# Moving the first loads of three phases of a training-step kernel into the last step of the phase before

## The chip, the cores and the metric

The kernel runs on one core of one Trainium2 chip. The metric is device time in microseconds (us), lower is better. Executions of one kernel spread by 10 to 20 us here (0.3 to 0.6%), so ratios come with a 95% interval and small claims rest on several executions. The engines are TensorE (PE in the profile, PEld for its weight loads), VectorE (DVE), ScalarE (ACT), GpSimd (POOL) and SyncE (SP).

## The reference, cut to what matters

The kernel computes the forward output and all gradients of one block: attention over segments with a memory carried from segment to segment, and a gated linear unit (GLU), both modulated by six vectors made from `c`.

```python
# 2048 rows of 512, 32 heads of 128, segments of 32 rows with 8 memory rows, F = 1792
for s in range(64):                                  # sequential
    h = concat([mem, xs]); q, k, v = h @ Wq, h @ Wk, h @ Wv
    o = softmax(mask(q @ k.T * scale)) @ v @ Wo
    mem = o[:8]; outs.append(o[8:])
x = x + ga * attention;  h = layernorm(x) * (1 + cb) + sb
x = x + gb * ((sigmoid(h @ w_gate) * (h @ w_up)) @ w_down)
# ... and jax.vjp of all of it for grad_out: 11 gradients
```

## The kernel before

The phases that matter here: phase 2 is the forward recurrence (64 steps), phase 3 the GLU as a pipeline of seven stages over 16 blocks of 128 rows, followed by the GLU's weight gradients (14 chunks of dW_down, then dW_gate and dW_up). Phase 4 is the backward recurrence, phase 5 the remaining weight gradients, beginning with the one of Wo. I call the handovers seam 1 (phase 2 to the GLU), seam 2 (GLU pipeline to its weight gradients) and seam 3 (phase 4 to 5).

```python
# start of the GLU (seam 1); tiles lie in memory that phase 2 has given back
nc.sync.dma_start(w_down[:], ...)                    # 1.83 MB, as w_up and w_gate
ga_bc, sb_bc, cb1_bc, gb_bc = ...                    # four broadcasts of 256 KB
...
load(0)                                              # row block 0: ten small loads on SP
nc.sync.dma_start(w_up[:], ...); nc.sync.dma_start(w_gate[:], ...)
load(1)
self.run_pipeline(NT, [s0, s1, s2, s3, s4, s5, s6], deepest_first=True)
...
# weight gradients (seam 2)
nc.sync.dma_start(dbr[:], self.DBROWS...)            # rows of d(block), 2.1 MB
for fc in range(FC):                                 # 14 chunks of 16 matmuls
    if fc % 3 == 0: hr = ...; nc.sync.dma_start(hr[...], self.HHROWS...)
    ...
# phase 5 (seam 3)
for tl in range(2):
    q = (nc.sync, nc.scalar)[tl]
    q.dma_start(rows_a[...], self.OSR...)            # 0.64 MB
    q.dma_start(dyrows[...], self.DAROWS...)         # 1 MB
    for tp_ in range(M // 2): q.dma_start(dyrows[...], DHA piece)
    q.dma_start(dyrows[last row], zrow)              # a row of zeros
```

The softmax here doesn't subtract the row's maximum and nothing guards it: scores larger than these inputs give would overflow.

## Time and profile before

| measured | before |
|---|---|
| median of 3 runs | 3368.5 us (3366.07 to 3373.47) |
| PE busy | 3056.8 us, 91% of the span |
| DVE, ACT, POOL busy | 49%, 36%, 31% |
| bytes moved by DMA | 692.22 MB, mean 205 GB/s |
| mean granted TensorE clock | 0.980 |

PE fills the kernel. The few dips lie at the seams, and the change addresses just those. The views that show it stand in the prediction. In the instruction view the bracket at the end of a line is the idle time of that engine just before the instruction, and what ended it.

### The profile page before, as it was taken

How to read it: one execution, taken by the hardware profiler on the slowest of the kernel's cores; microseconds unless marked ns; L12 is line 12 of the kernel's file. 1: busy time of each engine (PE TensorE's matmuls, PEld its weight loads, DVE VectorE, ACT ScalarE, POOL GpSimd, SP SyncE). 2: the span in 40 equal slices, each digit the busy share in tenths (PEclk: the TensorE clock that was granted, in tenths of full speed). 3: DMA queues.
4: the chain of work that ended last, by engine and by line, in shares of the span. 5: the costliest groups of instructions: out<-in, count | busy, mean ns of one | idle time of the engine just before them, and what ended most of it. 6: DMA issues, size and time to landing. Idle time of an engine off the chain costs nothing. (4 is left out here: it accounts for less than half of the span.)

```text
span 3368.5 us, 97290 instructions
## 1 busy us (share of the span) xinstructions
PE 3056.8 (91%) x39586; PEld 1793.4 (53%) x39662; DVE 1649.4 (49%) x4158; ACT 1225.1 (36%) x2842; POOL 1060.2 (31%) x2262
## 2 busy tenths in 40 slices
PE   6999999998998689978989999999999978999999
PEld 3566656565565444435555555555555543445454
DVE  5566666666665677633244455555544541322221
ACT  3454544444444333312134444444444430100111
POOL 2344433333343355530122222222222221322321
PEclk8999999999999899989999999999999998999999
DMA  8777787778777888877769999999999998777686
GB/s 281 154 168 161 165 156 163 155 158 157 155 162 154 215 204 206 197 214 248 229 178 242 240 245 236 250 244 242 246 240 244 241 235 226 236 195 210 179 225 164
DMA packets 862317, 692.22 MB, mean 205 GB/s; under 512 B 562198, under 2 KB 737574, under 8 KB 861740
## 3 DMA queue, kind: packets, MB, share of 16 engines
q1 hardware_dynamic: 768156, 503.74, 66.8%
q0 software_dynamic: 39488, 135.58, 12.0%
q10 hardware_dynamic: 54224, 46.66, 5.3%
q8 instruction: 312, 5.11, 0.6%
q14 instruction: 137, 1.12, 0.1%
HBM read 292.29 MB, written 275.02 MB: 168 GB/s over the span
## 5 line engine op out<-in xcount | busy, mean ns | idle before, releaser
L1584 PE MATMUL gps<-rows,hrows 128*128 128x512 bf16 (+2 forms) x2124 | 415.1, 355 | 1.9
L1584 PEld LDWEIGHTS <-hrows 128*128 128x128 bf16 x2160 | 211.2, 98 | 204.2
L222 PEld LDWEIGHTS <-hT 128*32 128x32 bf16 x6144 | 180.5, 98 | 174.1 <-issue 41.2
L65 POOL COPY vT<-b_colsv 128x24 bf16<-128x24 bf16 (+2 forms) x256 | 49.5, 238 | 577.6 <-DMA VT<-vT 569.1
L63 DVE CAST ot<-gps 128x512 bf16<-128x512 f32 (+3 forms) x77 | 48.9, 635 | 359.7 <-PE gps L1584 210.8
L272 DVE TENSOR_TENSOR dh_lo<-dh_ps,dh_hi 128x256 bf16<-128x256 f32 x128 | 48.3, 419 | 316.2 <-ACT dh_hi L268 316.2
L61 ACT ACTIVATE ot<-gps 128x512 bf16<-128x512 f32 (+3 forms) x77 | 42.5, 551 | 389.2 <-PE gps L1584 278.6
L737 POOL TENSOR_TENSOR Pst<-Pst,rden 120x1408 bf16<-120x1408 bf16 x64 | 162.3, 2535 | 36.3 <-POOL hT L481 20.7
L1588 POOL DMA_DIRECT2D out_dram<-ot x108 | 81.2, 752 | 290.3 <-DVE ot L63 155.2
L222 PE MATMUL pass_ps<-Wv,hT 128*32 128x512 bf16 x2048 | 127.2, 391 | 29.7 <-ACT hT L731 29.7
L1317 POOL DMA_DIRECT2D DVR<-rows_x x64 | 34.5, 540 | 371.6 <-DMA rows_x<-dVT 371.6
L222 PE MATMUL pass_ps<-WoT,dyT 128*32 128x512 bf16 x2048 | 125.1, 386 | 27.9 <-ACT dyT L1400 26.9
L61 ACT ACTIVATE dQT<-g_ps 128x512 bf16<-128x512 f32 (+1 forms) x192 | 94.0, 562 | 151.4 <-issue 146.5
L1594 PE MATMUL gps5o<-dyrows,rows 128*128 128x512 bf16 x588 | 134.5, 387 | 0.8 <-issue 0.2
L651 DVE TENSOR_TENSOR Ost<-or_ps,rden 120x512 bf16<-120x512 f32 (+1 forms) x192 | 124.3, 647 | 19.6 <-PE dc_ps L628 0.5
L1296 DVE SCALAR_TENSOR_TENSOR dS<-dp_ps,Pst_l 128x512 bf16<-128x512 f32 (+1 forms) x192 | 118.2, 643 | 24.1 <-PE dp_ps L1294 19.5
L222 PE MATMUL pass_ps<-Wk,hT 128*32 128x512 bf16 x2048 | 124.4, 383 | 0.0
L222 PE MATMUL pass_ps<-Wq,hT 128*32 128x512 bf16 x2048 | 122.4, 379 | 0.0
L211 PE MATMUL at_ps<-Wo,OT 128*32 128x512 bf16 x2048 | 122.3, 380 | 0.0
L211 PE MATMUL dh_ps<-WkT,dKT 128*32 128x512 bf16 x2048 | 122.3, 380 | 0.0
L211 PE MATMUL dh_ps<-WvT,dVT 128*32 128x512 bf16 x2048 | 122.2, 380 | 0.0
L211 PE MATMUL dh_ps<-WqT,dQT 128*32 128x512 bf16 x2048 | 121.6, 379 | 0.0
(383 smaller groups left out, 7106.9 us busy)
## 6 DMA issues: line engine op xcount, KB each, us to landing
OSR<-Ost SPq DMA_DIRECT2D x64, 352.0 KB
OT<-OT SPq DMA_DIRECT2D x64, 352.0 KB
PS<-Pst SPq DMA_DIRECT2D x64, 352.0 KB
OT_l<-OT SPq DMA_DIRECT2D x64, 352.0 KB
Pst_l<-PS SPq DMA_DIRECT2D x64, 352.0 KB
DVR<-rows_x POOLq DMA_DIRECT2D x64, 352.0 KB, 4.3
DKR<-rows_x POOLq DMA_DIRECT2D x64, 352.0 KB, 4.9
DQR<-rows_x POOLq DMA_DIRECT2D x64, 352.0 KB, 3.6
```

Of the source, the lines that this page charges most:

```text
L61: return nc.scalar.activation(out, in_, AF.Copy)
L63: return nc.vector.tensor_copy(out, in_)
L65: return nc.gpsimd.tensor_copy(out, in_)
L211: self.nc.tensor.matmul(ps[32 * j:32 * j + 32, :], lhsT=lhsT, rhs=w, start=(n < 4), stop=(n >= total - 4), tile_position=(0, 32 * j))
L222: self.nc.tensor.matmul(ps[32 * j:32 * j + 32, :], lhsT=lhs(c), rhs=rhs, start=(c == 0), stop=(c == DC - 1), tile_position=(0, 32 * j))
L272: nc.vector.tensor_tensor(lo[:], ps[:, 256 * h:256 * h + 256], parts[h][:], op=ALU.subtract)
L651: nc.vector.tensor_tensor(part3(Ost, pi)[0:120, 0:n, :], or_ps[0:120, 0:n, :], rden[:, pi * PG:pi * PG + n].unsqueeze(2).to_broadcast([120 ...
L737: nc.gpsimd.tensor_tensor(Pst[0:120, :, :], Pst[0:120, :, :], rden[:, :].unsqueeze(2).to_broadcast([120, G, 128]), op=ALU.mult)
L1296: nc.vector.scalar_tensor_tensor(out=part3(dS, pi), in0=ps[:, 0:n, :], scalar=cfg.scale, in1=part3(Pst, pi), op0=ALU.mult, op1=ALU.mult)
L1584: nc.tensor.matmul(ps[:, 0:ng * E], lhsT=hrows[:, tp_, c * 128:(c + 1) * 128], rhs=rows[:, tp_, 0:ng * E], start=(tp_ == 0), stop=(tp_ == ...
L1588: nc.gpsimd.dma_start(outw[c * 128:(c + 1) * 128, h0:h0 + 3 * (ng - 1) + 1:3, :], ot[:, 0:ng * E].rearrange("p (h e) -> p h e", e=E))
L1594: nc.tensor.matmul(ps[:], lhsT=rows[:, tp_, gg * E:(gg + 1) * E], rhs=dyrows[:, tp_, :], start=(tp_ == 0), stop=(tp_ == NTP - 1))
```

## The change

Its intent: no phase should begin with PE waiting for a first load. It lays the new phase's tiles over tiles of the old one that die early in its last step (`flat` makes such a view), and issues the loads as soon as the last reader is done. The core of the diff, cut:

```diff
# phase 2, last step: the GLU's weights over Wv and Wk
+                if s == NS - 1:                          # after the v projection
+                    nc.sync.dma_start(self.w_up, ...)
+                    self.mod_bc(None, 2, ...); self.mod_bc(None, 3, ...)
...
+                if s == NS - 1:                          # after the k projection
+                    nc.sync.dma_start(self.w_down, ...); self.mod_bc(None, 4, ...)
...
+                if s == NS - 1:                          # after q, k, v are turned
+                    self.mod_bc(None, 5, ...); nc.sync.dma_start(self.w_gate, ...)
...
+                if s == NS - 1:
+                    self.glu_first = self.glu_load(0, nc.scalar)    # row block 0 on ACT's queue
# GLU: three chunks of dW_down beside the drain of the pipeline
+            def after(it):
+                if it == NT + 1: nc.scalar.dma_start(dbr, ...)      # over w_gate and w_up
+                elif it == NT + 2: load_hr(0)
+                elif NT + 3 <= it < NT + 6: wd_chunk(it - NT - 3, ...)
# phase 4, last step: rows of phase 5 over WoT
+                if s == 0:
+                    self.p5_first()      # rows_a and the DAROWS part of dyrows, all on SP
...
             store_rows_x(0)
+            self.p5_second()             # the eight DHA pieces; zero rows stay in phase 5
```

## The prediction

> **What bounds the kernel now.** I read the page first: the busy slices show a kernel that TensorE (PE) fills, with a few dips, and each dip lies where one phase hands over to the next. The two lines that carry this are
>
> ```profile
> PE   6999999998998689978989999999999978999999
> PEclk8999999999999899989999999999999998999999
> ```
>
> A slice is 3368.5 / 40 = 84.2 us. Slice 13 (1095 to 1179 us) has PE at 6 and a lower granted clock: the handover from the forward recurrence (phase 2) to the GLU (phase 3). The handover from the GLU pipeline to its weight gradients (1477 to 1504) lies at the edge of slices 17 and 18, and that from the backward recurrence (phase 4) to the last weight gradients (phase 5) in slice 32 or 33. The change touches nothing else, so I went next to the engines' busy time in just those stretches:
>
> ```profile
> core 0: us, PE busy (x) PEld busy (x) DVE busy (x) ACT busy (x) POOL busy (x), PEclk, DMA share, GB/s
> 1109.00:1122.00 13.00, 5.41 (x52) 4.98 (x53) 3.84 (x11) 1.83 (x2) 1.64 (x3) 0.61 0.84 277
> 1122.00:1139.00 17.00, 9.11 (x128) 8.47 (x126) 11.38 (x19) 9.17 (x10) 3.63 (x5) 0.80 0.77 271
> 1170.00:1440.00 270.00, 248.12 (x1223) 116.58 (x1235) 186.01 (x314) 91.50 (x165) 153.54 (x161) 0.98 0.82 202
> 1477.00:1504.00 27.00, 8.10 (x45) 3.55 (x45) 8.65 (x16) 3.85 (x6) 6.67 (x9) 0.75 0.98 297
> 2769.00:2787.00 18.00, 0.41 (x2) 0.17 (x3) 0.80 (x5) 0.00 (x0) 0.54 (x1) 0.55 1.01 191
> 2787.00:2830.00 43.00, 37.13 (x151) 15.81 (x154) 7.21 (x15) 2.49 (x4) 6.63 (x11) 0.87 1.00 273
> ```
>
> In the steady GLU stretch (third row) PE works 248 of 270 us. In the handovers no compute engine is the bound; the DMA engines are (share 0.77 to 1.01), and PE waits for a first load. The instructions in order of time name each wait; the number in brackets is PE's idle time just before the line.
>
> ```profile
> 1117.52 5.41 PE L803 MATMUL tp<-ident,w_down 128*128 128x128 bf16 x56 [6.83 <-DMA w_down<-in_B_w_down_dram]
> 1129.38 4.19 PE L792 MATMUL tp<-ident,w_up 128*128 128x128 bf16 x48 [6.45 <-DMA w_up<-in_B_w_up_dram]
> 1139.16 0.93 PE L878 MATMUL mm<-w_gate,hdT 128*128 128x448 bf16 x4 [1.17 <-DMA hdT<-h]
> ...
> 1490.58 0.60 PE L979 MATMUL tp<-ident,da 128*128 128x128 bf16 x4 [5.29 <-DVE da L966]
> 1492.59 0.59 PE L975 MATMUL acc_ps<-pr_ga,ones 128*32 128x512 bf16 x1 [1.42 <-POOL pr_ga L969]
> 1503.99 12.34 PE L1024 MATMUL gps<-dbr,hr 128*128 128x512 bf16 x47 [10.78 <-DMA hr<-HHROWS]
> ...
> 2786.59 1.86 PE L1594 MATMUL gps5o<-dyrows,rows5a 128*128 128x512 bf16 x4 [17.60 <-DMA dyrows<-zrow]
> ```
>
> The sums: seam 1 has 6.83 + 6.45 + 1.17 = 14.5 us of waiting; seam 2 has 1.36 (before s5 of the last row block, for its transposed du) + 5.29 + 1.42 + 10.78 = 18.9; seam 3 has 17.6. Together 51.0 us, 1.5% of the time. That is the ceiling for waits alone.
>
> **What the Trainium skill says.** "TensorE: Matmul & The Clock Gate", section "What's actually happening": PE's default state is throttled, it falls back after an idle window of about 3.4 us and needs about as long of work to be released. The trace agrees: after the 17.6 us wait the granted clock is 0.55 and the first gradient matmuls run slowly. 47 recorded (48 issued) matmuls take 12.34 us after the wait at 1504, where a later run takes 4.48 us for 20, so 48 warm ones would take about 10.5. Each wait of over 4 us thus costs near 2 us more, and new waits would too. "DMA: Bandwidth & Descriptors", section "Queues, rings and completion order": each DMA engine consumes one queue's descriptors in ring order and takes turns between queues. So an early bulk load stands ahead of everything issued later on the SP queue. That agrees with w_up and w_gate: issued at 1121.9 and 1122.4, they landed at 1129.4 and 1134.2, one after the other, 3.67 MB in 12.3 us = 298 GB/s. I use that rate below. No page I found gives the wait I see on SP itself: its 9th transfer (1117.49) is issued only when the first of the eight before it (w_down) has landed, and the 10th when the second has. I take a depth of eight as this trace's behaviour.
>
> **The change, part by part.**
>
> *Seam 1.* The three GLU weights (1.83 MB each) and four 256 KB broadcasts are issued in the last step of phase 2, over Wv, Wk, Wq as soon as that step's projections have read them; row block 0 comes over the ACT queue. Removed: the waits on w_down and w_up. Not removed: the 168 transposes of the weights, which become PE's own limit. 112 of them took 1129.4 to 1138.0 = 8.6 us with both weights there; the other 56 are half, 4.3. From PE's last work of phase 2 (1110.7) this gives 1110.7 + 12.9 = 1123.6 at the earliest for the first GLU matmul, against 1139.16. A second chain is worse. The softmax transpose of the last step (Pst, issued at 1099 and landed by 1105.9) now goes into the SP queue behind the weights. From w_up's issue at about 1093: 5.5 + 1.0 + 0.9 MB (that step's own stores) at 298 GB/s = 25 us, so Pst lands near 1118 to 1121. GpSimd is held to program order there: the 2.5 us normalisation of Pst, three row stores (0.58 + 1.07), then rstd of block 0 (0.56), then VectorE's three operations to h2 (0.55 + 0.69 + 0.69), then the transposing DMA (issued at 1136.57, used at 1139.16: 2.6). Sum from 1119.5: 2.5 + 1.7 + 0.6 + 1.9 + 2.6 = 9.3, so 1129. Gain between 15.6 and 10; ten DMA issues on ScalarE (0.4 to 0.5 us each) before its last fold evictions cost up to 2. I take **10**.
>
> *Seam 2.* Three of the 14 dW_down chunks (48 matmuls) move into the drain of the pipeline, with dbr and the first hr group loaded over the dead w_gate and w_up from about 1454 on. Warm they take 10.4 us. Chunk 0 fits before s5(15), chunk 1 in the 5.3 us wait for da, chunk 2 after the last sums. Chunk 0 takes 3.5 us where only 1.4 was idle, so s5(15) and what hangs on it slip about 2 us. The next group hr(1) lies over cb1 and the a_rows ring, so it can't be issued before GpSimd's pr_ga(15) has read a_rows: 1492.5 + 2 to 3.5. It then needs the 8.1 us that hr(0) needed (1495.90 to 1503.99). So chunk 3 starts at about 1503 to 1504, where chunk 0 stands now; the three chunks' 12.2 us are gained, but the cold start (about 1.9) is paid again there. Gain **10**.
>
> *Seam 3.* rows_a and the DAROWS part of dyrows (2 x 0.64 + 2 x 1 MB) are issued at the start of step 0 over WoT, the eight DHA pieces at its end, and only two zero rows are left. Before, these stood behind the out_dram stores on SP (which wait for dh_rb at 2767) and behind each other. 3.4 MB from 2743.5 at 298 GB/s end at 2755; the DHA pieces follow by about 2765, the zero rows before 2770. PE ends phase 4 at 2769. Against me: the step's rows_x transpose now queues behind 2 MB, GpSimd's tail copies wait behind its store, and the tail's matmuls (2759.3) may slip 2 us. Start about 2771 instead of 2786.6, a gain of 15.5, plus some of the 2.2 us of cold clock (40 matmuls in 10.84 us, 8.65 warm). But 2787 to 2830 runs with DMA at share 1.00, and PE waits 4.78 us in it for a load. Only the 3.4 MB moved out (11 us), plus loads that can be issued sooner, speed that stretch. I count **14**.
>
> After each seam the kernel runs on PE as before, so the gains add: 10 + 10 + 14 = 34 us, 3368.5 - 34 = **3334 us** (0.990).
>
> **Rivals.** (a) *All waits vanish with the cold clocks*: 51 + about 6 gives 3311. For it: PE is the bound elsewhere (413 us busy of the 415 from 2945 on). Against it: the rings lie over live buffers (hr(1)), and the weight transposes are work. (b) *The moved loads only change places*: Pst and rows_x behind bulk transfers hold up GpSimd, and seams 1 and 3 gain 3 and 8. With 8 at seam 2 that is 3349. For it: DMA at 0.84 to 1.11 around all seams. Against it: rows_x and Pst feed no matmul of their own step. (c) *Overlaid views make false waits in the GLU's steady loop*, since the rings and w_down share one tensor: if loads waited for all readers of Wk, a row block (20 us) would grow by several us, and 16 of them by 50 or more: about 3385. Against it: the kernel before already fills and reads parts of tiles such as dyrows independently.
>
> **Range and chances.** Central 3334; (a) and (b) set the range, 3317 to 3353. A gain of 2% needs 67 us, more than all waits and cold clocks counted here, so faster gets 0.03; (c) or an upset instruction order gives slower 0.02; within 2% 0.95.
>
> **What would show it.** Right: waits on w_down and w_up gone and the first w_gate matmul 12 to 15 us after PE's last phase-2 work was due, or later with hdT, rstd or Pst named (the second chain); three dW_down chunks between 1477 and 1500 and a wait on hr of 4 to 7 us after them; the wait before the first gps5o under 4 us. Wrong: PE's time per GLU row block off 20 us, the stretch after gps5o's start losing what the start won, or any seam gaining under 4 us.

## More of the kernel before

The builder schedules: within one engine it may emit an instruction earlier than its place in the source where its data allow it. The recurrences are pinned to program order, the rest is not.

## The result, and the profile after

| | before | changed |
|---|---|---|
| median in the same rounds | 3370.54 us (4 runs) | 3357.61 us (3355.77 to 3365.03, 4 runs) |
| ratio | 1 | 0.9967, 95% interval 0.9947 to 0.9986 |
| profiled execution: span, clock | 3368.5, 0.980 | 3355.7, 0.983 |

A ratio here is the mean time of one kernel's fast runs over that of the other's fast runs of the same rounds, so it is not quite the ratio of the medians. The class "within 2%" was right, the number was not: 34 us were predicted, 13 came by the medians, and the time lies above the range's end of 3353.

The same two rows of the page of the changed kernel (40 slices of the span, busy tenths of PE and the granted clock in tenths):

```profile
PE   6999999999998699988989999999999988999999
PEclk8999999999999899999999999999999998999999
```

The dip at slice 17 is nearly gone (slices 16 to 19 read 9789 before and 9889 now), the one in slice 13 is still a 6, and seam 3 shows as two 8s in slices 32 and 33. So one seam of three looks mended. Busy time per stretch of the changed kernel, with stretches chosen to answer to those shown of before:

```profile
1106.00:1120.00 14.00, 0.00 (x0) 0.00 (x0) 0.43 (x1) 0.30 (x2) 0.00 (x0) 0.63 0.89 302
1120.00:1141.00 21.00, 14.37 (x179) 12.76 (x180) 15.65 (x29) 11.49 (x14) 11.29 (x12) 0.83 0.59 164
1485.00:1512.00 27.00, 18.54 (x100) 8.39 (x100) 8.90 (x17) 4.75 (x8) 8.40 (x12) 0.95 0.98 287
2752.00:2776.00 24.00, 7.67 (x106) 3.20 (x106) 1.51 (x6) 0.66 (x2) 4.27 (x9) 0.70 0.99 195
2776.00:2820.00 44.00, 39.22 (x160) 16.65 (x161) 8.41 (x20) 2.20 (x4) 5.54 (x9) 0.89 1.00 251
```

Columns: stretch, length, busy time and instructions of PE, PEld, DVE, ACT and POOL, then granted clock, DMA share, GB/s. First row: for 14 us at seam 1 the compute engines do almost nothing (PE 0, VectorE 0.43, ScalarE 0.30 us), while the DMA engines run at 302 GB/s. Third row: PE now works 18.5 of 27 us at seam 2, where before it worked 8.1. Last two rows: seam 3 still has the DMA engines at a share of 0.99 and 1.00, as before (1.01 and 1.00). PE's waits in order of time:

```profile
1120.14 0.21 PE L281 MATMUL ao_b_ft<-foldsel,ao_b_hi 128*128 128x32 bf16 x1 [14.81 <-ACT ao_b_hi L268]
...
1140.79 1.67 PE L909 MATMUL mm<-Wv,hdT 128*128 128x448 bf16 x4 [3.70 <-DMA hdT<-h]
...
1485.74 3.63 PE L1031 MATMUL mm<-Wv 128*128 128x512 bf16 x16 [0.98 <-DMA Wv<-HHROWS]
...
1512.20 5.41 PE L1031 MATMUL gps<-Wv,Wk 128*128 128x512 bf16 x16 [7.18 <-DMA Wk<-HHROWS]
...
2762.43 3.22 PE L211 MATMUL dh_tps<-WvT,dh_tail 128*32 128x512 bf16 x32 [10.60 <-POOL dh_tail L1732]
...
2776.37 11.66 PE L1673 MATMUL gps5o<-WoT 128*128 128x512 bf16 x40 [4.67 <-DMA WoT<-zrow]
...
2792.44 26.23 PE L1673 MATMUL gps5o<-WoT,rows 128*128 128x512 bf16 x113 [4.41 <-DMA rows<-OSR]
```

**Seam 1.** The waits for w_down and w_up are gone, and a new one of 14.81 us stands before phase 2's own last folding: PE waits for ScalarE. (w_gate shows as Wv, since it lies there.) Why ScalarE and GpSimd were late is in their own lines, from two views of that kernel, ScalarE's first (`db` is a product of the GLU's first blocks, `rstd` a factor of the layer norm, which `hdT` needs):

```profile
1104.76 0.41 ACTq L788 DMA_DIRECT2D Wk<-in_grad_out_dram  x1
1107.83 0.56 ACTq L319 DMA_DIRECT2D Wk<-AOA  x1
1113.45 0.28 ACTq L320 DMA_DIRECT2D Wk<-AOB  x1
1116.76 0.30 ACTq L319 DMA_DIRECT2D Wk<-AOA  x1
...
1119.70 0.66 ACT L268 ACTIVATE ao_b_hi<-ao_tps 128x256 bf16<-128x256 f32 x2 [17.48 <-DMA Wk<-AOB]
```

```profile
1126.81 2.53 POOL L760 TENSOR_TENSOR Pst<-Pst,rden 120x1408 bf16<-120x1408 bf16 x1 [21.67 <-DMA Pst<-ET]
...
1130.95 2.65 POOL L865 TENSOR_TENSOR db<-Wk,Wq 128x512 bf16<-128x512 bf16 x2
...
1134.68 0.58 POOL L878 TENSOR_TENSOR rstd<-ve,mhalf 128x1 f32<-128x1 f32 x1
```

The ten loads of row block 0 take ScalarE 0.3 to 0.6 us each to issue, but between the first four it stands still: the second, third and fourth start 3.1, 5.6 and 3.3 us after the one before. In the order of the built program every transfer on SP and ACT takes one of eight completion counters in turn, shared by the two queues (in the trace the semaphores 101 to 105, 108, 109 and 118 go round the transfers of both), and is not issued until the transfer that had it last has landed. SP stood in the same way: it issued w_gate at 1114.07 and Pst's transpose only at 1123.10. The early loads of block 0 therefore waited for weights and broadcasts, and ScalarE's last evictions of phase 2 waited behind them.

**Seam 2** went nearly as predicted: chunk 0 before the last block's products, a wait of 7.18 us on the next rows, just over the 4 to 7 predicted.

**Seam 3.** The 17.6 us wait is now 4.67 us, but 10.60 us stand in phase 4's own tail (PE waits for GpSimd's `dh_tail` copies) and 4.41 us a chunk later. SP's lines of that seam, in the changed kernel:

```profile
2740.20 5.83 SPq L1494 DMA_DIRECT2D WoT<-DAROWS  x1
2746.14 11.00 SPq L1379 DMA_TRANSPOSE rows_x<-dVT  x1
```

The issue of one small transposing load takes 11.00 us behind the bulk loads; the 192 loads of its kind in this trace take 1.98 us in the median, and no other over 3.9. GpSimd's store waits for that transpose, and its tail copies stand behind the store.

### The profile page after: what moved, and what is told of

It reads as the page before. It is cut to its first block, busy times and chain, and to the rows that moved or that the text cites. A ratio compares the mean times of both kernels' runs of the same rounds, so it can differ in the third digit from the quotient of the medians.

```text
span 3355.7 us, 97380 instructions
## 1 busy us (share of the span) xinstructions
PE 3060.2 (91%) x39662; PEld 1791.3 (53%) x39662; DVE 1644.5 (49%) x4158; ACT 1225.7 (37%) x2842; POOL 1061.3 (32%) x2262
## 5 line engine op out<-in xcount | busy, mean ns | idle before, releaser
L222 PE MATMUL pass_ps<-Wv,hT 128*32 128x512 bf16 x2048 | 126.0, 388 | 29.7 <-ACT hT L752 29.7
L1673 PE MATMUL gps5o<-WoT,rows 128*128 128x512 bf16 x600 | 134.2, 385 | 4.4 <-DMA rows<-OSR 4.4
```

The costliest lines, as they stand in the source:

```text
L222: self.nc.tensor.matmul(ps[32 * j:32 * j + 32, :], lhsT=lhs(c), rhs=rhs, start=(c == 0), stop=(c == DC - 1), tile_position=(0, 32 * j))
L1673: nc.tensor.matmul(ps[:], lhsT=rows[:, tp_, gg * E:(gg + 1) * E], rhs=dyrows[:, tp_, :], start=(tp_ == 0), stop=(tp_ == NTP - 1))
```

## The experiments

To compare traces I use marks in PE's instruction view: the last row transpose of phase 2 (of `at_tp`; the folding of the rows before comes after it in some traces), the first sum `pr_ga` of the GLU, the first and the last projection matmul against WoT in phase 4, and PE's last instruction. Stretch 1 (first to second mark) holds seam 1, stretch 2 (second to third) seam 2, stretch 3 (fourth to last) seam 3 and phase 5. Unless said otherwise, times are medians of four runs, with the kernel before in the same rounds.

### The change once more, and seam 1's two suspects

**c0_control** is the changed kernel again, with no edit.

> The changed kernel itself, run again as a control. All theories expect 3355 to 3359 us. From its trace I want to know which of the small shifts are the run's own: in the changed kernel's first trace the last row transpose of phase 2 stood 3.2 us earlier than before though nothing ahead of it was changed. If that is the run's own, it moves by some us here; the waits at the seams (14.8 us for the fold eviction on ScalarE, 7.2 for hr, 10.6 for the tail copies) should come again within 1 us.

Measured: 3356.77 us, ratio 0.9958 (0.9928 to 0.9987). The gain is real and of the size first seen. In its trace the waits for hr (7.56 us) and the tail copies (10.08) came again within 1 us, that for the fold eviction on ScalarE did not (11.52 for 14.81), and the last row transpose lay 2.6 us later with no edit.

**e1_block0_pool** takes ScalarE out of the issuing.

```diff
-                    self.glu_first = self.glu_load(0, nc.scalar)
+                    self.glu_first = self.glu_load(0, nc.gpsimd)
```

> Row block 0 of the GLU is loaded over GpSimd's queue, which has completion semaphores of its own, instead of ScalarE's, which shares eight with SP. Theory A (ScalarE stalled in its ten DMA issues because the bulk loads hold the shared semaphores, and that stall is what seam 1 lost): PE's 14.8 us wait for the fold eviction falls under 2 us, the first GLU matmul comes 5 to 12 us sooner after the last row transpose of phase 2 (35.7 us now), and the time is 3346 to 3352. Theory B (the chain Pst, GpSimd normalisation, rstd, h2, hdT ends as late anyway): the wait turns into one on hdT, the first matmul comes within 2 us of where it was, and the time is 3355 to 3358. In this order Pst's semaphore is no longer the one that w_gate holds, so B allows some gain if Pst is issued sooner.

**e2_gate_after_pst** issues w_gate behind Pst's transpose (Pst holds the last step's softmax weights; GpSimd normalises them before its work for the GLU).

```diff
-                    nc.sync.dma_start(self.w_gate, ...)      # after the VT store
...
                 nc.sync.dma_start(Pst[:], ET[:, :], transpose=True)
+                if s == NS - 1:
+                    nc.sync.dma_start(self.w_gate, ...)
```

> Only the load of w_gate moves: it is issued behind the transpose of Pst instead of ahead of it; ScalarE keeps the loads of row block 0. Theory A: PE still waits about 15 us for the fold eviction, and the time stays at 3355 to 3358. Theory B (Pst late, GpSimd held): Pst lands 6 to 10 us sooner, rstd and hdT follow, the first GLU matmul comes up to 5 us sooner if PE's transposes allow it; time 3352 to 3356. If both chains are about equally late, this alone gives nothing.

**e3_both** is e1 and e2 together.

> Both edits. If the two chains are parallel and about equally late (theory C), only this one gives the whole gain of seam 1: first GLU matmul 22 to 28 us after the last row transpose (35.7 now, 30.9 in the kernel before), time 3343 to 3349. Theory A: as the run with GpSimd's queue alone. Theory B: as the run with w_gate moved alone.

Measured: 3360.2, 3357.06 and 3362.03 us (ratios 0.9969, 0.9955, 0.9971, all intervals 0.4 to 0.5% wide). None beats the control in time. In the traces the first w_gate matmul comes 32.0, 29.8 and 33.1 us after the last row transpose, against 34.0 in the control. In e1 ScalarE's hold is gone, and in e2 Pst reaches GpSimd 11.6 us after the mark (18.5 in the control): both suspects were really there. But in e2 ScalarE is still held for 15.10 us, and its w_gate matmul is the earliest of the three, so that ScalarE's hold cost time is not shown; and theory C (22 to 28 us in e3) falls. In e1 and e3 a third hold stood behind the two. VectorE and PE in e3:

```profile
1117.03 0.43 DVE L813 TENSOR_SCALAR Wk<-Wk 128x512 f32<-128x512 f32 x1 [12.57 <-DMA Wk<-MODROW]
```

```profile
1117.85 0.21 PE L281 MATMUL ao_b_ft<-foldsel,ao_b_lo 128*128 128x32 bf16 x1 [10.78 <-DVE ao_b_lo L272]
```

The addition of 1 to the cb1 broadcast stands at the head of the GLU in the source, the builder placed it before phase 2's last VectorE evictions, and it waits for a broadcast queued behind w_down. VectorE kept to its order here, so the one wait of 12.57 us held the evictions behind it.

### Seam 1 undone, seam 3's order, and another queue

**u1_seam1_undone** emits the GLU's loads at the GLU's start again, in the order of before, with the overlaid tiles kept.

```diff
-                if s == NS - 1:
-                    nc.sync.dma_start(self.w_up, ...)          # and so for all of seam 1
...
+            nc.sync.dma_start(w_down, ...)                     # at the start of the GLU
+            for i in (2, 3, 4, 5):
+                self.mod_bc(None, i, "", t=self.bcs[i])
...
             load(0)
+            nc.sync.dma_start(w_up, ...); nc.sync.dma_start(w_gate, ...)
             load(1)
```

> The GLU's first loads (three weights, four broadcasts, row block 0) go back to the start of the GLU phase on the SP queue, in the order of the kernel before; the overlaid tiles, seam 2 and seam 3 stay as changed. Theory A (seam 1 as built loses about 11 us by the time the GLU pipeline is full: 4.8 to the first w_gate matmul and 6 in the fill): the first w_gate matmul comes about 31 us after the last row transpose of the forward recurrence (30.9 before, 34 to 35.7 in the change), the last sum pr_ga of the GLU comes 6 to 11 us earlier than in the change by that measure, and the time is 6 to 11 us below the changed kernel's 3357, at 3346 to 3351. Rival B (what seam 1 loses is run noise or comes back in the steady loop): the time stays within 3 us of the changed kernel.

Measured: 3351.6 us, ratio 0.9954 (0.993 to 0.9978); first w_gate matmul 30.9 us after the last row transpose. In number this is theory A, but it is not the undoing that I meant: SP's line shows that the builder moved w_gate (issued at 1089.35) and w_down (1094.96) into the last step by itself, since the overlaid tiles were free. It is one more order of early loads, and Pst's transpose was held 11.45 us behind those two.

**e5_bulk_after_turns** issues seam 3's bulk loads behind step 0's transposes and the DHA pieces.

```diff
-                if s == 0:
-                    self.p5_first()
...
             self.p5_second()
+            self.p5_first()
```

> Seam 3 only: the four bulk loads over WoT are issued behind step 0's own row transposes and the eight DHA pieces instead of ahead of them. Theory C (the 11 us issue of the rows_x transpose behind the bulk loads holds SP, then the DVR store, then the tail copies on GpSimd, and so PE's 10.6 us wait for dh_tail): that wait goes, the first output-projection gradient matmul comes 31 to 35 us after the last projection matmul against WoT (41.7 in both runs of the change, 45.3 before), and the time falls by 5 to 10 us. Rival D (the DMA engines are full, share about 1.1 from 2700 to 2800, so bytes only change places): PE starts earlier, but waits as much longer for the rows of the next chunks or for the bulk itself, and the time stays within 3 us of the changed kernel.

Measured: 3360.86 us, ratio 0.9982 (0.9966 to 0.9998). PE's lines:

```profile
2773.99 3.60 PE L1673 MATMUL gps5o<-WoT 128*128 128x512 bf16 x8 [18.14 <-DMA WoT<-OSR]
2780.02 9.94 PE L1673 MATMUL gps5o<-WoT 128*128 128x512 bf16 x32 [2.44 <-DMA WoT<-DAROWS]
```

The wait for `dh_tail` is gone, as theory C said, and PE then waits 18.14 us for the bulk itself. The start is 42.9 us after the last projection matmul (41.8 in the change). This is rival D, "bytes only change places". The transpose that was held for 11.00 us is issued in 1.40 here, with the bulk behind it.

**e6_both_cb1_late** is e3 with the addition moved in the source.

```diff
-            nc.vector.tensor_scalar_add(cb1_bc, cb1_bc, 1.0)
...
+                if j == 0:
+                    nc.vector.tensor_scalar_add(cb1_bc, cb1_bc, 1.0)
                 h2a = sbp.tile(...)
```

> e3_both, and the addition of 1 to the cb1 broadcast moved from the head of the GLU phase to just before its first use. In e3 VectorE stood 12.57 us in program order before that addition, waiting for a broadcast that is queued behind w_down, with the last fold evictions of the forward recurrence behind it, and PE waited 10.78 us for them. Theory E (VectorE's place in line is the third hold at this seam): PE's fold of the last rows ends within 3 us of the last row transpose, and PE's first transposes then wait for w_down itself; the first w_gate matmul still waits for GpSimd's chain through Pst, so it moves only 0 to 4 us, from 33 to 29 to 33 us after the last row transpose. Rival F (the addition on VectorE was the bound of the whole seam): the first w_gate matmul moves by 8 us or more, to under 26.

Measured: 3351.26 us, ratio 0.9954 (0.9938 to 0.997); first w_gate matmul at 29.7 us, so F falls. But theory E was not tested: VectorE still stood 9.03 us before the addition, because the builder had again placed it early. f6 mends that.

**e7_bulk_on_pool** puts the bulk on GpSimd's own queue, with row block 0 on SP.

```diff
-                    nc.sync.dma_start(self.w_up, ...); self.mod_bc(None, 2, ...) ...
+                    nc.gpsimd.dma_start(self.w_up, ...); self.mod_bc(None, 2, ..., q=nc.gpsimd) ...
# the same for w_down, w_gate and the other broadcasts
-                    self.glu_first = self.glu_load(0, nc.scalar)
+                    self.glu_first = self.glu_load(0, nc.sync)
# and the addition as in e6
```

> Seam 1 with the three weights and four broadcasts issued on GpSimd's own DMA queue at the same places, row block 0 on SP, and the cb1 addition late as in e6. Theory G (what holds the seam is the SP and ACT issuing line: held issues and completion slots shared with the bulk loads): Pst's transpose issues at once, no compute engine waits over 4 us for a slot, the first w_gate matmul comes 15 to 24 us after the last row transpose, and the time falls 8 to 14 us below the changed kernel's, to about 3343 to 3349. Rival H (the DMA engines' bandwidth is the bound: 5.5 MB must land in any case): Pst or block 0 or w_down lands late all the same, the first w_gate matmul stays at 28 to 33 us, and the time changes by less than 4 us.

Measured: 3366.78 us, ratio 1.0007 (0.9985 to 1.0028): the whole gain is lost, and theory G falls. The edit did not do all that was meant: the addition to cb1 was placed early again. VectorE stood 11.04 us before it, with phase 2's last evictions behind, PE waited 11.66 us for them, and the last row transpose came at 1119.27, later than in any other trace. So the lost time can't be put down to the queue alone, and the first w_gate matmul, 28.4 us after that late mark, is no gain. SP's lines in e7, in which no weight stands in SP's queue:

```profile
1100.16 3.46 SPq L535 DMA_DIRECT2D QST<-RA1q  x1
1103.72 3.41 SPq L707 DMA_DIRECT2D VT<-vT  x1
...
1111.02 10.96 SPq L721 DMA_TRANSPOSE Pst<-ET  x1
```

The last of these took 3.16 us in the kernel before, with no bulk around, and 4.99 in the median of its 64 steps (at most 6.05). So this hold does not come from a place in a queue: it is there when the bulk stands in another one. This agrees with the Trainium skill, "DMA: Bandwidth & Descriptors", section "Issuing engines are not separate DMA queues": whichever engine starts them, transfers run on the same 16 DMA engines and interleave. And "Perfetto Trace Analysis", section "DMA Instruction — HWDGE (DVE, Sync)", says what the long issue is made of: the reported window starts when the semaphores are satisfied, and contains the wait for the descriptor generator, the generation itself and the sequencer's last semaphore push. By that page the 10.96 us are thus no semaphore wait; which of the parts it was, no run here tells.

### Repairs by order and by bytes

**e4_tail_first** puts GpSimd's tail copies ahead of the store that waits for the held transpose.

```diff
-                store_rows_x(2)
+                if s > 0:
+                    store_rows_x(2)
...
                 tail.collect(s % nseg_t, [dVT, dKT, dQT])
+                if s == 0:
+                    store_rows_x(2)
```

> Seam 3 only: in the last step of the backward recurrence GpSimd's tail copies are emitted ahead of the store that waits for the rows_x transpose; the bulk loads stay where the change put them. Theory C' (half of seam 3's lost gain is GpSimd's place in line): PE's 10 us wait for dh_tail goes, but the output gradient's first matmul then waits for the DHA pieces and the zero rows, which still queue behind the held transposes, and comes 37 to 40 us after the last projection matmul (41.7 in the change, 45.3 before); the time falls by 0 to 4 us. Rival (nothing but that wait held the start): 33 us or less, and the time falls by 6 to 9 us.

Measured: 3356.99 us, ratio 0.997 (0.9946 to 0.9995). PE's line:

```profile
2773.20 1.87 PE L1676 MATMUL gps5o<-WoT 128*128 128x512 bf16 x4 [22.42 <-DMA WoT<-zrow]
```

PE's tail work ended 24.8 us after the last projection matmul (37.1 in the change), and all of the gain and more became a wait of 22.42 us for the last small loads, which ended at 47.2 us after that matmul, later than expected. What follows took 570.4 us to the end (571.4 to 580.1 in ten traces of the change's seam 3), and the time did not move.

**e8_small_first** sends few bytes before many at seam 1.

```diff
# three broadcasts, row blocks 0 and 1: GpSimd's queue; w_up stays early on SP
+                    self.mod_bc(None, 4, "", t=self.bcs[4], q=nc.gpsimd)
...
                 nc.sync.dma_start(Pst[:], ET[:, :], transpose=True)
+                if s == NS - 1:
+                    nc.sync.dma_start(self.w_down, ...); nc.sync.dma_start(self.w_gate, ...)
+                    self.mod_bc(None, 5, "", t=self.bcs[5])
...
+                    self.glu_first = [self.glu_load(j, nc.gpsimd) for j in (0, 1)]
# h2a of block 0 as (cb1 + 1) * xhf in one instruction, the addition after it;
# the first three products db tied behind rstd of block 0 by a one-column copy
```

> Seam 1 re-ordered so that little bytes go before many: three broadcasts and row blocks 0 and 1 on GpSimd's queue, w_down and w_gate behind Pst's transpose on SP (w_up stays early), the fourth broadcast behind them, the addition to cb1 tied behind its first use, and GpSimd's first products tied behind rstd of block 0. Theory H (the DMA engines' backlog is what holds the small transfers, whatever queue they stand in; e7 showed an 11 us held transpose with no bulk in its own queue): Pst's transpose issues in under 5 us, no engine waits over 9 us at the seam, the first w_gate matmul comes 15 to 23 us after the last row transpose, and the time falls 7 to 14 us below the changed kernel's 3357. Rival (the 5.5 MB bound the seam in any order): 27 us or more, and less than 4 us of time.

Measured: 3362.89 us, ratio 0.9995 (0.9969 to 1.002), first w_gate matmul 40.2 us after the last row transpose: a clear miss. With w_up and some small loads in flight the VT store took 4.68 us to issue (at most 1.34 in the 63 steps before). Pst's transpose took 5.98, against 4.95 in the median of all steps, so this one was hardly held. w_down went out only at 1114.92, and PE got it at 1127.73. The rival's "27 us or more" is what came: what is put later in this seam is missed later.

**e9_h_late** takes bytes away instead. The rows of h, some 2.5 MB, are first used in the eleventh chunk of phase 5 (the expectation says tenth).

```diff
-                    if 1 <= i <= 2:
-                        load_h(i - 1)
+                    if 4 <= i <= 5:
+                        load_h(i - 4)
```

> The changed kernel with the loads of hrows, about 2.5 MB that are first used in the tenth chunk of the last phase, issued in its fifth and sixth chunk instead of the second and third. Theory I (from 2770 to 2850 the DMA engines are full, so what seam 3 starts earlier it waits for later): the waits of 5 and 8 us for rows and dhb between 2790 and 2850 mostly go, the stretch from the first output-gradient matmul to the end shrinks from 575 to 580 us to 567 to 572, and the time falls by 5 to 9 us. Rival (those waits come from the SP line's order and not from bytes): under 3 us.

Measured: 3351.33 us, ratio 0.9953 (0.9926 to 0.998), 6 us below the change's 3357; the ratios overlap. It was run at another time. The stretch from the first output-gradient matmul to the end is 571.5 us, as theory I said, but 571.4 was seen once with the change unedited too, so the case rests on the four traces with late rows in the table below. PE's lines (the wait for rows was 4.41 us in the change):

```profile
2775.68 1.87 PE L1673 MATMUL gps5o<-WoT 128*128 128x512 bf16 x4 [4.35 <-DMA WoT<-zrow]
...
2787.73 15.92 PE L1673 MATMUL gps5o<-WoT,rows 128*128 128x512 bf16 x71 [1.64 <-DMA rows<-OSR]
```

**e10_all** is e4, e8 and e9 together.

> e4, e8 and e9 together. If the three theories hold and their gains add: 12 to 25 us below the changed kernel's 3357, so 3332 to 3345, a ratio to before of 0.987 to 0.992. If the DMA engines' bytes bind at both seams in any order, it stays at 3350 to 3357.

Measured: 3364.51 us, ratio 1.0004 (0.9974 to 1.0034). e8's loss came again (42.4 us to the first w_gate matmul), and stretch 3 is 616.5 us. ScalarE's half of the rows of h went out early all the same (2761.6 to 2793.7, with the first gradient matmul at 2783.4), so e9's edit was not fully in force. The gains did not add.

### Which seam pays

By then stretch 1 had varied by 6 us between traces of kernels with the same seam 1, so I needed a second trace of before. **b1_before** is the kernel before, one run.

> The kernel before once more, for a second trace of it: the stretches between the marks (last row transpose of the forward recurrence to the first sum pr_ga of the GLU 84.1 us; from there to the first projection matmul of the backward recurrence 510.3; first to last of those 1038.6; from there to the end 618.9) should repeat within 3 us if one trace is enough to set the three seams against each other; if they differ by 5 us or more, only means over several traces may be compared.

Measured: 3364.21 us. Stretch 1 is 93.0 us, where the first trace had 84.1. The condition "differ by 5 us or more" is met: one trace against one trace says nothing about seam 1, and my first reading of the result ("seam 1 loses 11 us", which theory A rests on) was chance. Stretch 3 is 620.6 us. The 618.9 that the expectations give for the first trace is a slip of mine: the last view that I read must have ended at 3360 us, PE worked until 3364.1, and the stretch is 622.8. The line that made most of the difference in stretch 1, from b1, where the first trace waited 6.83 us for the same weights:

```profile
1120.08 1.14 PE L803 MATMUL tp<-ident,w_down 128*128 128x128 bf16 x9 [16.22 <-DMA w_down<-in_B_w_down_dram]
```

**f1_before_h_late** is e9's edit in the kernel before.

> The kernel before with nothing but the hrows loads moved from the second and third chunk of the last phase to the fifth and sixth. Theory I (the last phase starts in a stretch in which the DMA engines are full, so bytes taken out of it shorten it whoever loads first): the stretch from the last projection matmul to the end falls from about 619 to 612 to 615 us, the time by 4 to 8 us. Rival (e9's 6 us come from the change's earlier start, or from chance): under 2 us.

Measured: 3359.84 us, ratio 0.9968 (0.9933 to 1.0003). Stretch 3 is 614.0 us, against 622.8 and 620.6 in the two traces of before. Theory I holds in the stretch; in time the interval just includes 1. This edit of two lines has about the ratio of the whole change (0.9967), but less surely.

**f3_seam2_only** undoes seams 1 and 3, with the order pinned so that the builder takes nothing early.

```diff
# seam 1 as in u1, and
             load(1)
+            self.pin(self.i_seam)      # program order from phase 2's end to here
# phase 5's loads at its start on SP and ACT as before, and
+            self.pin(self.i_seam3)
```

> Of the change only seam 2 and the overlaid tiles stay: the GLU weights and broadcasts are issued after the forward recurrence (order pinned, so that the builder cannot take them early as it did in u1), and the wgrad rows after the backward recurrence, on both queues as before. Theory J (the whole gain of the change is seam 2; seam 1 costs about 5 and seam 3 gives 0 because the DMA engines carry the same bytes in the same busy stretch): at or up to 6 us below the changed kernel's 3357, so 3350 to 3358. Rival K (seams 1 and 3 do pay): 5 to 12 us slower than the changed kernel, 3362 to 3369.

Measured: 3379.66 us, ratio 1.0025 (0.9994 to 1.0057). Neither theory: it is slower than before. Stretch 2 is 501.8 us and so keeps seam 2's gain; stretch 1 is 95.4 and stretch 3 is 636.3. The pin itself costs: the zero rows, pinned behind all else, made PE wait 35.03 us. The kernel before is not pinned there. So this is no clean undoing, and only its stretch 2 counts.

**f6_e6_h_late** is e6 with the addition really late, and e9's edit. The addition now depends on its first use:

```diff
+                if j == 0:
+                    nc.vector.scalar_tensor_tensor(out=h2a[:], in0=cb1_bc[:], scalar=1.0, in1=xhf[:], op0=ALU.add, op1=ALU.mult)
+                    nc.vector.tensor_scalar_add(cb1_bc, cb1_bc, 1.0)
```

> e6 as it was meant (block 0 on GpSimd's queue, w_gate behind Pst's transpose, and the addition to cb1 made to depend on its first use, so that VectorE cannot stand before it early) together with the late hrows loads of e9. By the stretches of e6 and e9: VectorE's wait of 9 to 12 us at seam 1 gone, last row transpose to first pr_ga 78 to 83 us (89 mean of the change), last projection matmul to the end 611 to 616 (620 mean of the change): 9 to 17 us below the changed kernel's 3357, so 3340 to 3348. If seam 1 is bound by bytes as in e8, 3350 or more.

Measured: 3354.8 us, ratio 0.9952 (0.993 to 0.9975). Stretch 1 is 82.3 us and stretch 3 is 613.7, both as expected, but stretch 2 was 510.7 in that trace (501.9 in the mean of the other 15 with its code), and the time is 7 us above the range: it fell under the expectation's last sentence, 3350 or more.

**c1_change_again** is the changed kernel in five rounds, and **f7_best** is f6 with the dW_down chunks one iteration later:

```diff
-                elif NT + 3 <= it < NT + 6:
-                    wd_chunk(it - NT - 3, ...)
+                elif NT + 4 <= it < NT + 6:
+                    for fc in ((0,), (1, 2))[it - NT - 4]:
+                        wd_chunk(fc, ...)
```

> The changed kernel again, in more rounds, as the yardstick for the next run and for the size of the whole gain: 3354 to 3361 us, a ratio to before of 0.995 to 0.998. In its trace the stretch from the first pr_ga to the first projection matmul of the backward recurrence is 498 to 506 us (506 to 510 in three traces that have the seam of before), and the stretch from the last projection matmul to the end 616 to 622, as before.

> f6 with one thing more: the three dW_down chunks in the GLU's drain are emitted one iteration later (none, one and two instead of one each), so that chunk 0 no longer stands before the last block's products, where it waited 1 to 3 us for its rows and then ran on a cold clock (5.1 to 5.3 us instead of 3.6). If the three repairs add: first pr_ga about 82 us after the last row transpose (89 mean of the change), the drain 221 to 225 us (228 mean of the change), last projection matmul to the end 612 to 616 (620): 8 to 17 us below the changed kernel in the same call, about 3341 to 3350. Rival (each is within what the DMA engines and the clock give back elsewhere, as f6's 3355 suggests): less than 4 us below it.

Measured, six runs each: the change 3356.41 us, ratio 0.9971 (0.9948 to 0.9994), f7 3348.97 us, ratio 0.9951 (0.9932 to 0.997). The means are 3355.9 and 3349.1; from the spread of the six and six runs the difference of 6.8 has a standard error of 2.9. That lies between the two expectations of f7, 8 to 17 and under 4. The change's own trace missed two of its ranges by little: stretch 2 496.4 (498 to 506), stretch 3 615.2 (616 to 622). f7 is the fastest kernel in its median, below both the kernel before and the change, by 0.5% and 0.2%. Of its three repairs two show in the trace and one does not:

```profile
1113.62 3.98 PE L841 MATMUL tp<-ident,Wk 128*128 128x128 bf16 x42 [4.52 <-DMA Wk<-in_B_w_down_dram]
...
1126.08 4.93 PE L830 MATMUL tp<-ident,Wv 128*128 128x128 bf16 x56 [3.57 <-DMA Wv<-in_B_w_gate_dram]
1137.64 1.67 PE L913 MATMUL mm<-Wv,hdT 128*128 128x448 bf16 x4 [6.63 <-DMA hdT<-h]
...
1487.27 3.17 PE L973 MATMUL mm<-Wq,duT 128*128 128x512 bf16 x7 [7.80 <-DMA duT<-du]
```

At seam 1 ScalarE and VectorE are no longer held in their lines (GpSimd still waits 10.26 us for Pst): PE ends phase 2 within 3 us of the last row transpose (theory E, at last tested), and then waits for w_down, for w_gate, and last for hdT, the end of the chain through Pst. Stretch 1 is 85.4, stretch 3 is 610.4. At seam 2 the later chunk 0 gave nothing: PE waits 7.80 us for the transpose of du, with the rows of the chunks being loaded at that time, where the kernel before waited 1.36. From the 14th pr_ga to the first projection matmul it takes 228.8 us, against a mean of 227.7 with the chunks as changed and 234.5 in the three traces of the kernel before.

## Why the prediction was wrong

Over all traces with the same code in a stretch, in us (means worked out from the marks, with the range):

| stretch | before | as changed | predicted for the change |
|---|---|---|---|
| 1, seam 1 | 88.3 (84.1 to 93.0, 3 traces) | 89.6 (86.9 to 93.1, 6 traces) | 78 |
| 2, seam 2 | 508.4 (506.0 to 510.3, 3) | 502.4 (496.4 to 510.9, 16) | 498 |
| 3, seam 3 and phase 5 | 621.7 (622.8 and 620.6, 2) | 619.2 (615.2 to 623.1, 10) | 608 |
| 1 with w_gate behind Pst (e2) and block 0 on GpSimd's queue too (e3, e6, f6, f7) | | 84.1 (82.3 to 86.1, 5) | |
| 3 with the rows of h late | 614.0 (f1) | 612.5 (610.4 to 613.7; e9, f6, f7) | |

The last column is the mean of before less 10, 10 and 14.

**Seam 1, predicted 10, found none.** One failing step is "ten DMA issues on ScalarE (0.4 to 0.5 us each) before its last fold evictions cost up to 2". The issues themselves took what was said; with the standing between them they kept ScalarE from its next eviction for 17.48 us in all. I had read in the trace of before that SP's ninth transfer waits for the landing of the first, and had not asked which queues share that depth, nor what else ScalarE does after its loads.

The second failing step is the sum "so 1129": Pst was expected to land at 1118 to 1121, and GpSimd got it at 1126.81. The last part of that chain, after Pst, was too short as well: 9.3 us were reckoned to the first w_gate matmul, and it came after 14.0. Two products `db` with their stores (2.65 and 1.11 us) stood on GpSimd before rstd; one of them stands there in the trace of before too. The first w_gate matmul hangs on this step: PE's last wait before it is the one for hdT (3.70 us in the change).

e1 and e2 show both suspects, e3 a third (VectorE), and the five traces with w_gate behind Pst are 4 us below the mean of the kernel before in stretch 1, which its three traces (84.1 to 93.0) do not set clear of chance. e2, with ScalarE still held, is as low as f6 and f7 (84.1 for 82.3 and 85.4), so these traces give no cost to that hold. What bounds the rest is open: f7's PE waits 4.52 and 3.57 us for w_down and w_gate, and last 6.63 for hdT.

**Seam 2, predicted 10, found 6** (6.8 from the 14th pr_ga on, where the traces of before and of the change do not overlap). The steps held: the chunks in the drain, the slip of the last block, the wait on the next rows (4 to 7 us said, 7.1 to 7.6 in most traces). Mis-sized was the loss: chunk 0 waits up to 3.3 us for its rows, and after most of the waits of 2 us and more it runs slowly (5.1 to 5.3 us for 16 matmuls, once 6.6, instead of 3.6), so the last block slips by more than the 2 us said. The granted clock, which the prediction lowers only after the drain, fell within it: 0.68 over chunk 0 in c0, after a wait of 2.05 us (but 1.00 in e8, after 2.47).

**Seam 3, predicted 14, found 2.5, less than the spread.** Two steps failed. "The tail's matmuls may slip 2 us": they waited 10.60, through the held transpose and GpSimd's line, and PE ended phase 4 37.1 us after the last projection matmul instead of 27.7. That ate 9.4 of the 12.9 us by which the wait before the first gradient matmul shrank (17.60 to 4.67). The first gradient matmul came 42.3 us after the last projection matmul in the mean of ten traces, 44.6 in three of the kernel before: 2.3 us earlier, not 15.5. And "only the 3.4 MB moved out, plus loads that can be issued sooner, speed that stretch": from that matmul to the end it took 576.9 us in the mean of the ten, 577.1 in two traces of before. It was not sped up, and nothing was given back. e4 and e5 show that these two orders do not help. Both remove the wait for dh_tail, and PE waits 22.42 and 18.14 us instead for what was put later. e9 and f1 show what helps: loads that are not needed yet, taken out of the full stretch, give 7 us in stretch 3 with or without the change (the four traces of the table's last row lie below all others). They take bytes from the DMA engines and issues from SP's and ScalarE's lines; which of the two pays, no run separates.

**The rivals.** (c), false waits in the GLU's loop, did not come: blocks take 20.5 us at their steady pace in both kernels. (b) was nearest, "the moved loads only change places", but I gave it 3 and 8 us at seams 1 and 3, and took as an argument against it that "rows_x and Pst feed no matmul of their own step". That is true and beside the point: they hold GpSimd's line, in which the next matmul's operands are made. Of my warning signs, "any seam gaining under 4 us" came, at seams 1 and 3; "the stretch after gps5o's start losing what the start won" did not. Two readings of the prediction are off with little weight: the clock of 0.55 is that of the wait itself (the 43 us after it have 0.87), and 48 warm matmuls at 4.48 us for 20 take 10.8 us, not 10.5.

**What stays open.** The stretches account for 1.3 us lost, 6.0 and 2.5 us gained, some 7 us. The timed runs give 10 to 15 (means of the change's three sets of runs against before: 11, 15 and 10). The unchanged parts vary by more than that: the last row transpose of phase 2 lay between 1101 and 1111 us in most traces, at 1095 in e1 and 1119 in e7. No run here finds the rest of the gain. A clean undoing of seam 1 alone or of seam 3 alone was not measured (u1 and f3 are none).

## What to carry to other kernels

An early load is not free because its queue is idle: before moving it, ask what each engine that issues it or waits near it does next in its own line, and whether the DMA engines still have room in that stretch. At seam 3, where their share was near 1, taking out loads that were not yet needed gave 7 us, and two reorderings gave nothing. Where a builder schedules, check the built order of every moved instruction, since moving a line in the source may move nothing, and a pin may cost more than it tests. And take two or more traces of the same kernel before explaining a difference of a few microseconds between two kernels.

## What the Trainium skill lacked or had wrong

- "DMA: Bandwidth & Descriptors", section "Issuing engines are not separate DMA queues": right that another queue brings no more room (e7: a transpose held 10.96 us with the bulk on another queue; 4.99 us in the median without bulk). It calls the time to initiate a transfer usually small; that section lacks that the issuing engine's compute stands behind the issues and the waits between them. Ten loads issued on ScalarE kept it from its next evictions for 17.48 us.
- The same page, section "Queues, rings and completion order": it lacks that a small transposing load can be held in its issue by bulk already in flight (11.00 us in the change, against 1.40 in e5 with the bulk behind it; 11.45 in u1). "Perfetto Trace Analysis", section "DMA Instruction — HWDGE (DVE, Sync)", gives the parts of that window but no hint that they can reach 11 us.
- No page that I found has the turn of eight completion counters that the built program shares between SP and ACT here, so that a transfer on ScalarE waits for one on SP (3.1, 5.6 and 3.3 us from one issue to the next).
- No page that I found says how far a stretch varies between executions of one kernel: seam 1 of the kernel before took 84.1 and 93.0 us in two of them.
